# Loading order, transposes and output quotas at the start of a fused convolution and Swish layer

## Chip, cores, metric

One core of a Trainium2 chip; the calls of runs went to several chips. The metric is the device time of one execution in microseconds (us). The timeline is counted from the first instruction.

## Reference

Input x is 8 sequences of 4096 tokens with 192 features. A causal convolution of 7 taps, its weights a softmax per head, mixes tokens; then every token goes through a layer with 2048 hidden units.

```python
w = softmax(weight, axis=-1)                       # [8 heads, 7 taps]
conv[b, s] = sum_k w[head, k] * x_padded[b, s + k] # head = feature // 24
h = conv @ w_in                                    # [32768, 192] @ [192, 2048]
out = (h / (1 + exp(-beta * h))) @ w_out           # [2048, 192]
```

## The kernel before

Work comes in 32 stages. A stage takes one chunk of 512 tokens from each half of the batch. It has 16 units; each computes 128 hidden units for 2 x 512 tokens (6 matmuls into PSUM tile `ph`, then a Silu on ScalarE), and runs output matmuls for hidden units that are already done. Output work is cut into jobs: one job accumulates 256 tokens over all 16 units (32 pairs of matmuls) in a PSUM tile, `pa` or `pb`, and VectorE then reduces that tile to `osb` for the store. Two jobs at most are open, one per tile.

```python
def jobs_of(s):            # four jobs a stage: two batch halves x two token ranges
    ...
def output(s, u, pairs, free):
    for _ in range(pairs):
        for name in free:                       # "a" and "b": the two PSUM tiles
            if slots[name] is None and waiting:
                slots[name] = waiting.popleft()
        ...                                     # the oldest job that has something ready
        if job.pair():                          # two matmuls; true after the 32nd pair
            job.leave()                         # reduction on VectorE, store
            slots[name] = None
```

The convolution of chunk s+2 runs on VectorE during stage s, as 21 operations (taps) that are popped one or two at a time from a queue, between the reductions. It needs the chunk transposed, so a cast load on GpSimd writes the chunk as bf16 to DRAM (`cast`), and a DMA transpose brings it back as features x tokens (`xpose`).

```python
for s in range(N_ST):
    if s == 0:
        queue.extend(conv_ops(1, 1))
    jobs_of(s)
    for u in range(NF):                         # 16 units
        ...                                     # hidden(s, u)
        output(s, u, 8, "a" if s == 0 and u <= CONV1[-1] else "ab")   # CONV1 ends at 10
        ...                                     # pops_u taps from the queue
        if u == 0 and s + 4 < N_CH:
            cast(s + 4)
        if u == 1 and s + 2 < N_CH:
            xpose(s + 2)
            queue.extend(conv_ops(s + 2, 0))
```

The first two chunks are special. Chunk 0 is transposed on TensorE and convolved there. Chunk 1 is loaded, cast on VectorE and sent through four DMA transposes; one of its three column groups is then convolved on TensorE, tap by tap, in units 4 to 10 of stage 0. The casts of later chunks are let go by a small GpSimd copy that waits for the first convolved column of chunk 0:

```python
for b in range(NB):
    nc.sync.dma_start_transpose(
        xt[:, :, HALO + b * BLK : HALO + (b + 1) * BLK],
        x1b[:, b].rearrange("q c h d -> q (c h d)"),
    )
...
        if c == 0:
            nc.gpsimd.tensor_copy(hold, cts[0][0:1, 0, 0:1])
scale_w_out(0)
cast(2)
cast(3)
```

## Time and profile before

| | before |
|---|---|
| median of 3 runs (range) | 716.6 us (716.33 to 718.79) |
| span of the profiled execution | 717.9 us |
| TensorE busy | 695.2 us, 97% |
| stage 0 starts, stage 1 starts | 15.05, 42.29 us |
| last unit ends | 707.0 us |

Part 1 of the page of the kernel before, busy us by engine:

```profile
PE 695.2 (97%) x11320; PEld 521.0 (73%) x11320; DVE 522.5 (73%) x810; ACT 578.7 (81%) x532; POOL 59.6 (8%) x74
```

TensorE bounds it. In the timeline its pattern of 6 hidden and 16 output matmuls repeats every 1.307 us, with no gap, in all undisturbed units; 16 units make 20.92 us and 32 stages 669 us. So the question is where the remaining 49 us go. The two largest entries of what TensorE waited for, in all of the kernel before (us in total, times, longest):

```profile
PE pa L410 <- DVE osb L429: 9.8, 14, 1.1
PE pb L257 <- DVE xt L342: 4.9, 1, 4.9
```

And the two largest of VectorE:

```profile
DVE ct L362 <- DMA xt<-xd: 122.6, 26, 6.1
DVE osb L429 <- PE pa L410: 41.9, 19, 9.2
```

**The single wait of 4.9 us** is in stage 0. TensorE in the timeline of before (start, duration, engine, line, operation, then in brackets the idle time ahead of it and what ended it):

```profile
19.77 0.82 PE L380 MATMUL ph<-ct,w_in_s 64*128 64x512 bf16 x6
25.54 0.79 PE L257 MATMUL pb<-xt,diag 128*128 128x512 f32 x1 [4.94 <-DVE xt L342]
```

The tap needs chunk 1, whose DMA transposes were issued from 14.1 us; VectorE had the last of it at 24.8. The windows view of before for the same stretch (busy us of TensorE, weight loads, VectorE, ScalarE, GpSimd; then granted clock, DMA share, GB/s; the DMA share is the time of all packets over that of the 16 engines, and as packets overlap it can pass 1):

```profile
21.00:22.00 1.00, 0.00 (x0) 0.00 (x0) 0.00 (x0) 0.75 (x1) 1.00 (x2) 1.00 2.44 157
22.00:23.00 1.00, 0.00 (x0) 0.00 (x0) 0.00 (x0) 0.00 (x0) 1.00 (x2) 0.75 2.11 168
23.00:24.00 1.00, 0.00 (x0) 0.00 (x0) 0.00 (x0) 0.00 (x0) 1.00 (x2) 0.50 2.26 148
27.00:28.00 1.00, 1.00 (x7) 0.16 (x3) 1.00 (x3) 0.00 (x0) 0.17 (x1) 0.50 1.40 242
```

TensorE is idle, the DMA share is above 2, and the granted clock falls to 0.50 and stays there after work has resumed. The Trainium skill, "TensorE: Matmul & The Clock Gate", Part 1 ("The HAM clock gate"), says that an idle window of about 3.4 us puts the array at half clock. The trace agrees in part. The idle time here, 4.94 us, is longer than that and the clock did fall; but the windows view in steps of 0.25 us has it fall at 22.5 us, only 1.9 us after TensorE's last matmul (20.6).

**The 14 short waits** are at stage boundaries. VectorE, then TensorE, in the timeline of before, near the start of a later stage:

```profile
228.18 8.03 DVE L364 SCALAR_TENSOR_TENSOR ct<-xt,cw,ct 128x512 bf16<-128x512 bf16 x12
236.13 0.95 DVE L429 TENSOR_REDUCE osb<-pa 128x384 f32<-128x768 f32 x1
237.00 0.95 DVE L429 TENSOR_REDUCE osb<-pb 128x384 f32<-128x768 f32 x1
242.79 0.88 DVE L362 TENSOR_SCALAR ct<-xt,cw 128x512 bf16<-128x512 bf16 x3 [4.85 <-DMA xt<-xd]
```

```profile
235.18 0.83 PE L380 MATMUL ph<-ct,w_in_s 64*128 64x512 bf16 x6
237.14 0.84 PE L410 MATMUL pa<-w_out_s,g 64*128 64x192 bf16 x16 [1.12 <-DVE osb L429]
```

Two things meet. The jobs in `pa` and `pb` finish in the same unit, so both tiles wait for a reduction and the next job has none. And VectorE works in order (the same page, in the paragraph "Engine queue depths", calls it a strict FIFO; this trace agrees: the reductions start at 236.13 us, when the 12 taps of 8.03 us ahead of them are out): it had stood idle for a transpose at the start of the stage, was behind with its taps, and the reductions came late. Even a stage that shows no such wait takes 21.17 us, not 20.92. The DMA transposes of before, issued once a stage at the same place:

```profile
67.04 3.81 SPq L113 DMA_TRANSPOSE xt<-xd  x1
88.21 4.15 SPq L113 DMA_TRANSPOSE xt<-xd  x1
```

### The profile page before, as it was taken

The page shows a single profiled execution, that of the slowest core. Times are in us where ns is not written, and L with a number is a line of the kernel's source. Part 1 is how long each engine was busy: PE and PEld are TensorE (multiplying, and loading weights), DVE is VectorE, ACT ScalarE, POOL GpSimd, SP SyncE. Part 2 cuts the span into 40 slices and gives each one's busy share as a digit, 9 for nine tenths or more (in the row PEclk, how much of TensorE's full clock was granted, in tenths as well). Part 3 has the DMA queues.
Part 4 walks back from the last instruction along what each step waited for, and adds up shares of the span by engine and source line. Part 5 has one row for each costly group of instructions (what it writes and reads, how often), then busy time and mean ns, then how long its engine had stood idle before and what let it go on. Part 6 is the DMA issues. An engine that isn't in the chain of part 4 may idle for free.

```text
span 717.9 us, 24618 instructions
## 1 busy us (share of the span) xinstructions
PE 695.2 (97%) x11320; PEld 521.0 (73%) x11320; DVE 522.5 (73%) x810; ACT 578.7 (81%) x532; POOL 59.6 (8%) x74
## 2 busy tenths in 40 slices
PE   8799999999999999999999999999999999999997
PEld 5377777777777777777777777777777777777776
DVE  5588888987886777887766887667887677797321
ACT  5588888888888788887888888887888878888884
POOL 4555442000000000000000000000000000000000
PEclk9899999999999999999999999999999999999999
DMA  8999999522113222312223112332212322213111
GB/s 189 170 164 172 163 175 173 82 57 59 51 42 70 68 57 57 54 40 68 69 57 58 56 38 69 68 58 57 53 40 69 68 57 59 59 39 63 46 35 57
DMA packets 185784, 55.35 MB, mean 77 GB/s; under 512 B 148032, under 2 KB 185680, under 8 KB 185680
## 3 DMA queue, kind: packets, MB, share of 16 engines
q0 software_dynamic: 96544, 12.92, 27.5%
q1 hardware_dynamic: 89088, 40.85, 24.9%
q8 instruction: 88, 1.44, 0.9%
q14 instruction: 16, 0.13, 0.1%
q10 hardware_dynamic: 48, 0.01, 0.0%
HBM read 28.98 MB, written 37.29 MB: 92 GB/s over the span
## 4 chain that ended last, share of the span: by engine, by line
PE 37%; DVE 31%; DMA 24%; issue 4%; POOL 1%; SPq 1%; ACT 0%
DVE ct L364 22%; PE ph L380 17%; DMA xd<-in_x_dram 12%; DMA xt<-xd 11%; PE pa L410 10%; PE pb L410 9%; DVE osb L429 8%; DMA x<-in_x_dram 1%; DVE ct L362 1%; POOL xd L104 1%; SPq L437 1%; SPq L140 0%; ACT g L388 0%; DVE ct L318 0%; DVE x1b L299 0%
## 5 line engine op out<-in xcount | busy, mean ns | idle before, releaser
L388 ACT ACTIVATE g<-ph,beta 128x1024 bf16<-128x1024 f32 x512 | 570.2, 1114 | 121.5 <-PE ph L380 117.5
L410 PEld LDWEIGHTS <-g 64*128 64x128 bf16 x8192 | 368.0, 94 | 123.4 <-issue 22.7
L380 PE MATMUL ph<-ct,w_in_s 64*128 64x512 bf16 x3072 | 424.2, 377 | 0.3 <-ACT g L388 0.2
L364 DVE SCALAR_TENSOR_TENSOR ct<-xt,cw,ct 128x512 bf16<-128x512 bf16 x552 | 371.7, 745 | 0.0
L410 PE MATMUL pa<-w_out_s,g 64*128 64x192 bf16 x4128 | 240.6, 243 | 11.5 <-DVE osb L429 9.8
L410 PE MATMUL pb<-w_out_s,g 64*128 64x192 bf16 x4064 | 224.5, 243 | 0.0
L380 PEld LDWEIGHTS <-w_in_s 64*128 64x128 bf16 x3072 | 158.5, 94 | 54.3 <-issue 1.6
L362 DVE TENSOR_SCALAR ct<-xt,cw 128x512 bf16<-128x512 bf16 x92 | 27.8, 354 | 122.7 <-DMA xt<-xd 122.6
L429 DVE TENSOR_REDUCE osb<-pa 128x384 f32<-128x768 f32 x64 | 61.0, 954 | 41.9 <-PE pa L410 41.9
L429 DVE TENSOR_REDUCE osb<-pb 128x384 f32<-128x768 f32 x63 | 59.9, 950 | 10.2 <-PE pb L410 10.2
L104 POOL DMA_DIRECT2D xd<-in_x_dram x60 | 54.6, 912 | 45.0 <-DMA xd<-in_x_dram 43.3
L257 PE MATMUL pb<-xt,diag 128*128 128x512 f32 x7 | 4.1, 584 | 4.9 <-DVE xt L342 4.9
L257 PEld LDWEIGHTS pb<-xt,diag 128*128 128x128 f32 x7 | 1.5, 215 | 8.4 <-DVE xt L342 5.4
L257 PE MATMUL ph<-xt,diag 128*128 128x512 f32 x14 | 5.4, 562 | 0.1
L257 PEld LDWEIGHTS ph<-xt,diag 128*128 128x128 f32 x14 | 4.0, 294 | 1.5 <-ACT xt L271 0.5
L320 ACT ACTIVATE ct<-pa,rn 128x512 bf16<-128x512 f32 x1 | 0.7, 688 | 5.3 <-PE pa L257 5.3
L426 ACT COPY osb<-pb 128x192 f32<-128x192 f32 x1 | 0.3, 320 | 5.6 <-PE pb L410 5.6
L288 DVE TENSOR_TENSOR w_out_s<-w_out_raw,beta_r 128x768 bf16<-128x768 f32 x4 | 3.8, 954 | 0.9 <-DMA w_out_raw<-in_moe_w_out_dram 0.9
L342 DVE CAST xt<-xt 128x518 fp32r<-128x518 bf16 x1 | 0.7, 699 | 5.1 <-DMA xt<-x1b 5.1
L210 PE MATMUL ph<-zeros 128*128 128x512 bf16 x6 | 2.9, 623 | 1.3 <-DVE warm L154 1.3
L188 DVE COPY w_in_s<-w_in_s 64x1536 bf16<-64x1536 bf16 x4 | 2.7, 686 | 0.9 <-DMA w_in_s<-in_moe_w_in_dram 0.8
L350 DVE TENSOR_SCALAR ct<-pb,rn 128x512 bf16<-128x512 f32 x1 | 0.8, 751 | 2.9 <-PE pb L257 2.9
(54 smaller groups left out, 33.3 us busy)
## 6 DMA issues: line engine op xcount, KB each, us to landing
out_dram<-osb SPq DMA_DIRECT2D x127, 192.0 KB, 2.1
xd<-in_x_dram POOLq DMA_DIRECT2D x54, 198.0 KB, 14.7
w_out_raw<-in_moe_w_out_dram SPq DMA_DIRECT2D x4, 384.0 KB, 9.6
xd<-in_x_dram POOLq DMA_DIRECT2D x6, 192.0 KB, 11.1
x<-in_x_dram SPq DMA_DIRECT2D x4, 192.0 KB, 3.3
x<-in_x_dram SPq DMA_DIRECT2D x2, 384.0 KB, 9.1
w_in_s<-in_moe_w_in_dram POOLq DMA_DIRECT2D x4, 192.0 KB, 9.4
xt<-xd SPq DMA_TRANSPOSE x30, 4.7
```

The source lines that it names most:

```text
L104: nc.gpsimd.dma_start(out=xd[r0:, :, h, :], in_=x_v[p, t0:t1, h, :].rearrange("t (c d) -> t c d", c=NG),)
L188: nc.vector.tensor_copy(w_in_s[DG : 2 * DG, :, cols], w_in_s[0:DG, :, cols])
L210: nc.tensor.matmul(pf[:, 0, 0:cols], zeros[:, 0:128], zeros[:, 0:cols], start=True, stop=True)
L257: nc.tensor.matmul(pv, diag[:, c, k, :], xt[:, o : o + TOK], start=(k == 0), stop=(k == K - 1))
L288: nc.vector.tensor_tensor(w_out_s[:, fcs, :], w_out_raw[:, fcs, :], beta_r[:, fcs].unsqueeze(2).to_broadcast((128, NQ, D)), ALU.mult,)
L362: nc.vector.tensor_scalar_mul(dst, src, scalar)
L364: nc.vector.scalar_tensor_tensor(out=dst, in0=src, scalar=scalar, in1=dst, op0=ALU.mult, op1=ALU.add)
L380: nc.tensor.matmul(ph[:, h, :], w_in_s[rows, j, fc * 128 : (fc + 1) * 128], cts[s][rows, j, :], start=(j == 0), stop=(j == NG - 1),)
L388: nc.scalar.activation(gs[s][:, fc], ph, AF.Silu, scale=beta[:, fc : fc + 1])
L410: nc.tensor.matmul(self.po[:, r, b * D : (b + 1) * D], g[rows, fc, self.h, q * BLK : (q + 1) * BLK], w_out_s[rows, fc, :], start=(self.don ...
L429: nc.vector.tensor_reduce(dst, self.po[:, :, 0 : nb * D].rearrange("p r n -> p n r"), axis=mybir.AxisListType.X, op=ALU.add,)
L437: nc.sync.dma_start(out=out_v[self.h, p, t : t + nb * BLK, :].rearrange("(b q) d -> q b d", q=BLK), in_=osb[:, 0:nb, :],)
```

## The change

Its intent: get chunk 1 to TensorE sooner (transpose it there, not by DMA), load the first rows in longer pieces, keep other loads out of the way, and have later transposes done before VectorE asks for them. It also lowers the output quotas of stage 0. The core of the diff (cuts marked):

```diff
-    for b in range(NB):                                   # x0: four loads, 768-byte rows
-        nc.sync.dma_start(...)
+    def load_x(dst, t0):                                  # x0, x1: two loads each, 1536-byte rows
+        for i in range(2):
+            ...  "(q b) h d -> q h (b d)", b=2
...
-    for i in range(NW):
-        load_w_in(i)
+    load_w_in(0)
...                                                        # after the conv weights are spread:
+    nc.gpsimd.tensor_copy(hold[:, 0:1], eu[0:1, 0, 0:1])
+    for i in range(1, NW):
+        load_w_in(i)
...
-        nc.sync.dma_start_transpose(...)                  # chunk 1, four times
+    def second():                                         # chunk 1, in units 1 and 2; casts in unit 3
+        ...
+            for b in range(2):
+                transposes(halves[i][:, :, b], x1b, 2 * i + b)     # TensorE
+            nc.vector.tensor_copy(...)                             # PSUM to xt
+            ...
+        nc.gpsimd.tensor_copy(hold[:, 1:2], xt[0:1, 0, HALO + TOK - 1 :])
+        cast(2)
+        cast(3)
...
-            output(s, u, 8, "a" if s == 0 and u <= CONV1[-1] else "ab")
+            if s > 0:
+                output(s, u, 8, "ab")
+            elif u > CONV1[-1]:
+                output(s, u, 5, "ab")
+            elif u > 2:
+                output(s, u, 3, "a")
...
-            if u == 1 and s + 2 < N_CH:
-                xpose(s + 2)
+            if u == 1 and s > 0 and s + 3 < N_CH:
+                xpose(s + 3)
+            ...                                           # stage 0: xpose(2) in unit 4, xpose(3) in unit 12
+            if u == 4 and s + 2 < N_CH:
                 queue.extend(conv_ops(s + 2, 0))
```

Not shown: two of the four `w_out` loads move forward, short `fill` matmuls are added at the start, and some weight copies change place.

More of the change, by code (lines that the diff above doesn't have):

```diff
@@ L120 @@
     NQ = NF // NW
-    x0 = setup.tile([128, NB, 2, D], FP32)
-    x1 = setup.tile([128, NB, 2, D], FP32)
+    x0 = setup.tile([128, 2, 2, 2, D], FP32)
+    x1 = setup.tile([128, 2, 2, 2, D], FP32)
     x0b = setup.tile([128, NB, NG, 2, DG], BF16)
@@ L138 @@
     nc.scalar.dma_start(out=cw8, in_=weight)
-    for b in range(NB):
-        nc.sync.dma_start(
-            out=x0[:, b, :, :], in_=x_v[0, b * BLK : (b + 1) * BLK, :, :]
-        )
-    for h in range(2):
-        nc.sync.dma_start(
-            out=x1[:, :, h, :],
-            in_=x_v[0, TOK : 2 * TOK, h, :].rearrange("(b q) d -> q b d", q=BLK),
-        )
-    load_w_out(0)
-    load_w_out(1)
+    def load_x(dst, t0):
+        for i in range(2):
+            t = t0 + i * 2 * BLK
+            nc.sync.dma_start(
+                out=dst[:, i].rearrange("q h b d -> q h (b d)"),
+                in_=x_v[0, t : t + 2 * BLK, :, :].rearrange(
+                    "(q b) h d -> q h (b d)", b=2
+                ),
+            )
+    load_x(x0, 0)
+    load_x(x1, TOK)
+    for i in range(NW):
+        load_w_out(i)
     zeros = setup.tile([128, TOK], BF16)
@@ L214, with spread, cast_rows, transposes @@
     NK = NG * (K + 1)
-    def spread(dst, sel, e8):
-        for c in range(NG):
-            nc.tensor.matmul(
-                dst[:, c * (K + 1) : (c + 1) * (K + 1)],
-                sel[:, c, :, :].rearrange("i h d -> i (h d)"),
-                e8,
-                start=True,
-                stop=True,
-            )
+    def spread(dst, sel, e8, c):
+        nc.tensor.matmul(
+            dst[:, c * (K + 1) : (c + 1) * (K + 1)],
+            sel[:, c, :, :].rearrange("i h d -> i (h d)"),
+            e8,
+            start=True,
+            stop=True,
+        )
+    def cast_rows(xb, x, b):
+        nc.vector.tensor_copy(
+            xb[:, b].rearrange("q c h d -> q h c d"),
+            x[:, b // 2, :, b % 2].rearrange("q h (c d) -> q h c d", c=NG),
+        )
+    def transposes(pt, xb, b):
+        for c in range(NG):
+            nc.tensor.transpose(
+                pt[:, c, :], xb[:, b, c].rearrange("q h d -> q (h d)"), ident_b
+            )
+    def tokens(xt, b):
+        t = HALO + (b // 2) * 2 * BLK
+        return xt[:, :, t : t + 2 * BLK].rearrange("p c (q b) -> p c b q", b=2)[:, :, b % 2]
     fill(5)
     pc = in_a()
-    spread(pc[:, 0, :], sel_r, e8r)
+    for c in range(NG):
+        spread(pc[:, 0, :], sel_r, e8r, c)
+        fill(1, 256)
     for b in range(NB):
-        nc.vector.tensor_copy(
-            x0b[:, b].rearrange("q c h d -> q h c d"),
-            x0[:, b].rearrange("q h (c d) -> q h c d", c=NG),
-        )
+        cast_rows(x0b, x0, b)
     eu = setup.tile([128, NG, K + 1], FP32)
     nc.vector.tensor_copy(eu.rearrange("p c k -> p (c k)"), pc[:, 0, 0:NK])
+    hold = setup.tile([1, 2], FP32)
+    nc.gpsimd.tensor_copy(hold[:, 0:1], eu[0:1, 0, 0:1])
+    for i in range(1, NW):
+        load_w_in(i)
     diag = setup.tile([128, NG, K, 128], FP32R)
@@ L266 @@
         pt = pts[b % 2][:, b // 2, 0 : NG * BLK].rearrange("p (c q) -> p c q", c=NG)
-        for c in range(NG):
-            nc.tensor.transpose(
-                pt[:, c, :], x0b[:, b, c].rearrange("q h d -> q (h d)"), ident_b
-            )
-        nc.scalar.copy(xt0[:, :, HALO + b * BLK : HALO + (b + 1) * BLK], pt)
+        transposes(pt, x0b, b)
+        nc.scalar.copy(tokens(xt0, b), pt)
+        fill(1, 128)
     pb = pc[:, 1, 0:NF]
@@ L295 @@
     copy_w_in(0)
-    xt = new_xt(1)
-    for h in range(2):
-        nc.vector.tensor_copy(
-            x1b[:, :, :, h, :], x1[:, :, h, :].rearrange("q b (c d) -> q b c d", c=NG)
-        )
-    nc.vector.tensor_copy(xt[:, :, HALO - PAD : HALO], xt0[:, :, HALO + TOK - PAD :])
-    for b in range(NB):
-        nc.sync.dma_start_transpose(
-            xt[:, :, HALO + b * BLK : HALO + (b + 1) * BLK],
-            x1b[:, b].rearrange("q c h d -> q (c h d)"),
-        )
-    load_w_out(2)
-    load_w_out(3)
-    hold = setup.tile([1, 1], BF16)
     new_ct(0)
@@ L321 @@
         if c == 0:
-            nc.gpsimd.tensor_copy(hold, cts[0][0:1, 0, 0:1])
-    scale_w_out(0)
-    cast(2)
-    cast(3)
+            for b in range(NB):
+                cast_rows(x1b, x1, b)
     cw = consts.tile([128, NG, K], FP32)
-    def taps():
+    def second():
+        xt = new_xt(1)
+        pt = in_b()
+        halves = [
+            pt[:, i, 0 : NG * BLK].bitcast(BF16).rearrange(
+                "p (c b q) -> p c b q", c=NG, b=2
+            )
+            for i in range(2)
+        ]
+        for i in range(2):
+            for b in range(2):
+                transposes(halves[i][:, :, b], x1b, 2 * i + b)
+            t = HALO + i * 2 * BLK
+            nc.vector.tensor_copy(
+                xt[:, :, t : t + 2 * BLK].rearrange("p c (q b) -> p c q b", b=2),
+                halves[i].rearrange("p c b q -> p c q b"),
+            )
+            if i == 0:
+                nc.vector.tensor_copy(
+                    xt[:, :, HALO - PAD : HALO], xt0[:, :, HALO + TOK - PAD :]
+                )
+                scale_w_out(0)
+            yield
+        nc.gpsimd.tensor_copy(hold[:, 1:2], xt[0:1, 0, HALO + TOK - 1 :])
+        cast(2)
+        cast(3)
         pq = in_b()[:, 0, 0:NK]
-        spread(pq, sel, e8)
+        for c in range(NG):
+            spread(pq, sel, e8, c)
         pq = pq.rearrange("p (c k) -> p c k", c=NG)
+        copy_w_in(1)
         rq = setup.tile([128, NG], FP32)
@@ L338, in taps @@
         )
+        yield
     def conv1():
@@ L474, in output @@
                 slots[name] = None
+    second_work = second()
     conv1_work = conv1()
     first_work = {
-        1: lambda: (copy_w_in(1), scale_w_out(1)),
+        4: lambda: scale_w_out(1),
         5: lambda: copy_w_in(2),
@@ L499 @@
                     hidden(0, fc, range(NG - 1, NG), phs[fc])
-            else:
-                taps()
+            if s == 0 and 0 < u < 4:
+                next(second_work)
             if s == 0 and u in CONV1:
                 next(conv1_work)
-            output(s, u, 8, "a" if s == 0 and u <= CONV1[-1] else "ab")
+            if s > 0:
[4 more added lines that the diff above has]
+                output(s, u, 3, "a")
             if s == 0 and u in first_work:
@@ L514 @@
                     queue.popleft()()
-            if u == 0 and s + 4 < N_CH:
+            if u == 0 and s > 0 and s + 4 < N_CH:
                 cast(s + 4)
-            if u == 1 and s + 2 < N_CH:
-                xpose(s + 2)
+            if u == 1 and s > 0 and s + 3 < N_CH:
+                xpose(s + 3)
+            if s == 0 and u == 4:
+                xpose(2)
+                cast(4)
+            if s == 0 and u == 12:
+                xpose(3)
+            if u == 4 and s + 2 < N_CH:
                 queue.extend(conv_ops(s + 2, 0))
```

## The prediction

> **What bounds it now.** TensorE: the page gives it 695.2 of 717.9 us busy (97%). In an undisturbed stage the timeline shows one unit (6 hidden, 16 output matmuls) every 1.307 us; the Silu needs 1.11 us (groups). 16 units are 20.92 us, so 32 stages have a floor of 669 us; the rest is start, tail and waits.
>
> **Where time is lost.**
> 1. Start. The timeline has TensorE idle from 20.6 to 25.5 us (waits: "DVE xt" 4.9 us): the second chunk goes through four DMA transposes (issued 14.1, landed 24.8) while loads hold the DMA share above 1.4 (windows). The granted clock is then 0.50 for some 6.8 us. The Trainium skill, "TensorE: Matmul & The Clock Gate", Part 1, says an idle window of about 3.4 us halves the clock; this trace agrees. Stage 0 starts at 15.05, stage 1 at 42.3.
> 2. Stage boundaries. Vector idles 122.6 us in 26 waits for xt<-xd, because the transpose is issued just before its taps enter Vector's in-order queue; it then runs 12 taps without a break (8.0 us), and the PSUM reductions come late. Two output jobs also finish in the same unit of every stage, so the next must wait for a reduction. Waits list 9.8 us in 14 for "PE pa <- DVE osb", up to 1.1 us. The good stages too take 21.17 us, not 20.92 (transpose issues), 0.25 us lost at this place. From stage 1 to the end of the last unit (707.0) it takes 664.7 us for 31 stages, 16.2 us over 31 x 20.92.
>
> **What changes.**
> - x0/x1: larger rows, fewer issues, three w_in loads held back: stage 0 starts near 14.3.
> - Second chunk: 12 TensorE transposes (about 0.17 us each, partly in Silu-bound units, nearly free), two Vector copies of about 0.9 us. Vector should have xt1 near 21.3, so a stall of about 1.5 us stays, likely too short to lose the clock. Units 5 to 10 stay at 1.35 us; units 11 to 15 carry 5 output pairs, not 8, so near 1.1 us. Stage 1 starts near 36.0: gain 6.3 us.
> - The 15 output pairs not done in stage 0 move to the tail: +1.3 us at 0.088 us each, partly returned by a lost 0.7 us reduction wait there: +0.4 net.
> - Transposes a stage sooner, taps entering at unit 4, and, through the changed backlog, reductions at units 0, 2, 6, 10 (instruction order): no two adjacent, each over two units before its bank is wanted. I expect 15.7 of the 16.2 us back.
> Vector is not the limit (16.5 of 21 us a stage).
>
> **Sum.** Span 717.9 - 6.3 - 15.7 + 0.4 = 696.3; the unprofiled median lies 1.3 below: 695 us. Range 690.5 to 701. Chances: faster by over 2% 0.90, within 2% 0.09, slower 0.01.
>
> **What would show it.** Waits: "PE pa <- DVE osb" below 1.5 us; "DVE ct <- DMA xt<-xd" below 8 us, all near the start; transposes issued every 20.9 us; stage 1 near 36; clock at 1.00 from 22 to 29 us; tail about 11.4 us.
>
> **What would make it wrong.** Held-back w_in or the later casts (issued near 20, not 15 us) arrive late, and Vector, in order, blocks in stage 0 or on chunk 2: 2 to 4 us lost. The stall near 20 us stays long enough to halve the clock. Or the stage boundary has another limit than reductions: then a stage stays at 21.17 and the time is near 702.

## The result

697.66 us, median of 4 runs (696.41 to 698.47), against 717.69 (716.33 to 720.02) in 4 runs of before. The ratio is 0.9716, 95% interval 0.9683 to 0.9749. Ratios are computed as the mean time of one kernel's fast runs over that of the other's of the same rounds, so not quite the ratio of the medians. Later line numbers shift: L441, L411, L460, L393 after are L410, L380, L429, L362 before.

Part 1 of the page, after:

```profile
PE 688.6 (99%) x11339; PEld 497.9 (71%) x11339; DVE 528.2 (76%) x814; ACT 578.5 (83%) x532; POOL 60.6 (9%) x75
```

What TensorE waited for, after. The reductions are gone from the list, the wait for chunk 1 is down to 0.3 us (the last line), and a wait for beta is new:

```profile
PE pa L293 <- DMA beta_q<-in_moe_beta_dram: 1.4, 1, 1.4
PE ph L213 <- DVE warm L158: 1.3, 1, 1.3
PE ph L411 <- ACT g L419: 0.6, 1, 0.6
PE pa L441 <- ACT g L419: 0.4, 1, 0.4
PE pb L220 <- DVE xt L346: 0.3, 1, 0.3
```

What VectorE waited for, after. It now idles for its reductions' inputs, which costs nothing:

```profile
DVE osb L460 <- PE pa L441: 121.5, 61, 6.8
DVE ct L393 <- DMA xt<-xd: 0.2, 1, 0.2
```

TensorE around the first tap of chunk 1, after, and two of the same windows:

```profile
21.38 0.81 PE L411 MATMUL ph<-ct,w_in_s 64*128 64x512 bf16 x6
22.12 0.50 PE L279 MATMUL pb<-xt,diag 128*128 128x512 f32 x1
```

```profile
22.00:23.00 1.00, 1.00 (x11) 0.55 (x11) 1.00 (x2) 0.77 (x1) 1.00 (x2) 1.00 1.02 66
23.00:24.00 1.00, 1.00 (x9) 0.31 (x7) 0.97 (x2) 0.68 (x2) 1.00 (x2) 1.00 2.27 145
```

No wait there, and the clock stays at 1.00. The reductions in a later stage, after, are no longer neighbours of each other:

```profile
225.81 0.96 DVE L460 TENSOR_REDUCE osb<-pa 128x384 f32<-128x768 f32 x1 [0.85 <-PE pa L441]
226.68 2.07 DVE L395 SCALAR_TENSOR_TENSOR ct<-xt,cw,ct 128x512 bf16<-128x512 bf16 x3
228.67 0.95 DVE L460 TENSOR_REDUCE osb<-pb 128x384 f32<-128x768 f32 x1
```

And the transposes of after are issued every 20.92 us:

```profile
227.27 1.45 SPq L113 DMA_TRANSPOSE xt<-xd  x1
248.19 1.44 SPq L113 DMA_TRANSPOSE xt<-xd  x1
```

In sections, from the timelines of the two profiled executions:

| section | before | predicted | after |
|---|---|---|---|
| to the start of stage 0 | 15.05 | 14.3 | 15.58 |
| stage 0 | 27.24 | 21.7 | 20.60 |
| stages 1 to 31 | 664.7 | 649.0 | 648.7 |
| tail | 10.9 | 11.4 | 11.8 |
| span | 717.9 | 696.3 | 696.7 |

The span came out as predicted, in part because two errors cancel (see below). And the change bundles six edits, and two theories that share a total can differ on which edits earn it. The prediction itself credited the middle row to "transposes a stage sooner" and the backlog together, and the stage-0 row to the TensorE transposes. The experiments separate these.

### The profile page after: what moved, and what is told of

Read it like the earlier page. It is cut to its first block, busy times and chain, and to the rows that moved or that the text cites. A ratio compares the mean times of both kernels' runs of the same rounds, so it can differ in the third digit from the quotient of the medians.

```text
span 696.7 us, 24650 instructions
## 1 busy us (share of the span) xinstructions
PE 688.6 (99%) x11339; PEld 497.9 (71%) x11339; DVE 528.2 (76%) x814; ACT 578.5 (83%) x532; POOL 60.6 (9%) x75
## 4 chain that ended last, share of the span: by engine, by line
PE 98%; DMA 1%; ACT 0%; DVE 0%; issue 0%; ACTq 0%
PE ph L411 47%; PE pa L441 25%; PE pb L441 24%; DMA beta_q<-in_moe_beta_dram 1%; PE ph L279 1%; PE pb L279 0%; PE pa L279 0%; ACT g L419 0%; ACT L159 0%; DVE xt L346 0%; DVE w_out_s L308 0%; PE pb L220 0%; ACTq L138 0%; PE ph L213 0%; PE pb L237 0%
## 5 line engine op out<-in xcount | busy, mean ns | idle before, releaser
L441 PEld LDWEIGHTS <-g 64*128 64x128 bf16 x8192 | 352.3, 94 | 121.2 <-issue 1.7
L411 PE MATMUL ph<-ct,w_in_s 64*128 64x512 bf16 x3072 | 415.1, 376 | 0.6 <-ACT g L419 0.6
L395 DVE SCALAR_TENSOR_TENSOR ct<-xt,cw,ct 128x512 bf16<-128x512 bf16 x552 | 375.9, 745 | 0.0
L441 PE MATMUL pa<-w_out_s,g 64*128 64x192 bf16 x4128 | 234.1, 243 | 0.4 <-ACT g L419 0.4
L441 PE MATMUL pb<-w_out_s,g 64*128 64x192 bf16 x4064 | 224.5, 243 | 0.0
L411 PEld LDWEIGHTS <-w_in_s 64*128 64x128 bf16 x3072 | 141.9, 94 | 62.0 <-issue 0.9
L460 DVE TENSOR_REDUCE osb<-pa 128x384 f32<-128x768 f32 x64 | 61.3, 958 | 121.9 <-PE pa L441 121.5
L460 DVE TENSOR_REDUCE osb<-pb 128x384 f32<-128x768 f32 x63 | 60.0, 953 | 31.2 <-PE pb L441 31.1
L393 DVE TENSOR_SCALAR ct<-xt,cw 128x512 bf16<-128x512 bf16 x92 | 30.3, 359 | 0.2 <-DMA xt<-xd 0.2
L213 PE MATMUL ph<-zeros 128*128 128x512 bf16 (+2 forms) x13 | 5.3, 475 | 1.3 <-DVE warm L158 1.3
L346 DVE COPY xt<-pb 128x768 bf16<-128x768 bf16 x2 | 1.9, 958 | 2.6 <-PE pb L237 2.6
L213 PEld LDWEIGHTS <-zeros 128*128 128x128 bf16 x13 | 1.6, 129 | 2.2 <-DVE warm L158 1.3
```

The source lines that it names most:

```text
L213: nc.tensor.matmul(pf[:, 0, 0:cols], zeros[:, 0:128], zeros[:, 0:cols], start=True, stop=True)
L346: nc.vector.tensor_copy(xt[:, :, t : t + 2 * BLK].rearrange("p c (q b) -> p c q b", b=2), halves[i].rearrange("p c b q -> p c q b"),)
L393: nc.vector.tensor_scalar_mul(dst, src, scalar)
L395: nc.vector.scalar_tensor_tensor(out=dst, in0=src, scalar=scalar, in1=dst, op0=ALU.mult, op1=ALU.add)
L411: nc.tensor.matmul(ph[:, h, :], w_in_s[rows, j, fc * 128 : (fc + 1) * 128], cts[s][rows, j, :], start=(j == 0), stop=(j == NG - 1),)
L441: nc.tensor.matmul(self.po[:, r, b * D : (b + 1) * D], g[rows, fc, self.h, q * BLK : (q + 1) * BLK], w_out_s[rows, fc, :], start=(self.don ...
```

## Experiments

Kernels named `a_` are edits of the changed kernel, `b_` of the kernel before; `after_again` is the changed kernel itself. All twelve runs gave correct results. Medians are compared within one call (same chip, same rounds) where that is possible. The changed kernel itself ran only in the first and the last call, so its comparison with the other `a_` kernels crosses calls. The kernel before had medians of 717.7 to 720.7 us.

### Stage boundaries: quota or earlier transposes?

**a_quota8**

```diff
-                output(s, u, 5, "ab")
+                output(s, u, 8, "ab")
```

> The changed kernel, with 8 output pairs instead of 5 in units 11 to 15 of stage 0, everything else kept (early transposes, TensorE transposes, held loads). Theory BACKLOG (the backlog that the smaller quota leaves staggers the PSUM reductions, and that stagger is what removes the wait at stage boundaries): two reductions are adjacent again in every stage, each of 31 stages loses 0.25 us again (period 21.17, not 20.92), stage 0 is about 1.2 us longer and the tail about 0.6 us shorter: 704 to 706 us, about 7.5 over the changed kernel's 697.7; no stage loses over 0.4 us, because Vector isn't blocked by a transpose. Rival SOONER (only the earlier transposes matter): 697 to 699 us, period 20.92.

Measured: 705.14 us (704.77 to 705.47), ratio to before 0.9803. The transposes, still early, are issued every 21.17 us. VectorE and TensorE at a stage boundary of a_quota8:

```profile
206.42 0.96 DVE L460 TENSOR_REDUCE osb<-pa 128x384 f32<-128x768 f32 x1 [1.22 <-PE pa L441]
207.30 0.95 DVE L460 TENSOR_REDUCE osb<-pb 128x384 f32<-128x768 f32 x1
208.16 2.07 DVE L395 SCALAR_TENSOR_TENSOR ct<-xt,cw,ct 128x512 bf16<-128x512 bf16 x3
```

```profile
206.54 0.83 PE L411 MATMUL ph<-ct,w_in_s 64*128 64x512 bf16 x6
207.43 0.84 PE L441 MATMUL pa<-w_out_s,g 64*128 64x192 bf16 x16
208.09 0.83 PE L411 MATMUL ph<-ct,w_in_s 64*128 64x512 bf16 x6
```

The two reductions are neighbours again, though VectorE was idle and took the first at once. The next job starts when that reduction is out (206.42 + 0.96 = 207.38), and the unit takes 1.55 us, not 1.307. The waits view does not list this, because the modelled ends of the pipelined matmuls cover the gap; the start times show it.

**a_late**

```diff
-            if u == 1 and s > 0 and s + 3 < N_CH:
-                xpose(s + 3)
+            if u == 1 and s > 0 and s + 2 < N_CH:
+                xpose(s + 2)
+                queue.extend(conv_ops(s + 2, 0))
...
-            if s == 0 and u == 12:
-                xpose(3)
-            if u == 4 and s + 2 < N_CH:
+            if u == 4 and s == 0:
                 queue.extend(conv_ops(s + 2, 0))
```

> The changed kernel, with the transposes from stage 1 on issued as in the kernel before (chunk s+2 in unit 1 of stage s, its taps entering at the same place), the quota of 5 kept. BACKLOG: Vector idles again about 4 us a stage for the transposed chunk (over 100 us in all), but no TensorE wait comes of it, because each bank is free two units before it is wanted: 697 to 699.5 us, period 20.92. SOONER: the waits come back, 8 to 16 us more, 705 to 714 us.

Measured: 697.93 us (697.83 to 698.88), 0.3 us over the changed kernel's median. VectorE and TensorE waits of a_late:

```profile
DVE ct L393 <- DMA xt<-xd: 65.6, 27, 5.5
```

```profile
PE pa L441 <- DVE osb L460: 0.5, 1, 0.5
PE pb L441 <- DVE osb L460: 0.3, 1, 0.3
```

VectorE waits for transposes again (65.6 us, less than the 100 expected, because part of the time now goes to reductions that come in between: its waits for their inputs are 89.5 us, against 52.1 before). In this view TensorE loses 0.8 us by it. The start times show somewhat more: stages 5 and 6 take 22.09 and 21.21 us, together 1.5 us over twice 20.92, and no later stage loses anything. TensorE in stage 5 of a_late, behind the longest of VectorE's waits above (5.5 us, to 131.4):

```profile
132.94 0.42 PE L441 MATMUL pa<-w_out_s,g 64*128 64x192 bf16 x6 [0.49 <-DVE osb L460]
```

The transpose that VectorE waited for there was issued at 120.9 us, so it took 10.5 us, while casts were still running (the last landed at 133.5 us). The next four, with no casts left, took 3.9 to 5.1 us. The time of this execution (698.03 us, against 698.47 of the changed kernel's) does not show the 1.5 us, because its stage 0 started at 13.71 us and not at 15.58.

**b_quota5**: in the kernel before, only the output line is replaced by the six lines of the diff above.

> The kernel before, with only the output quotas of stage 0 changed (3 pairs up to unit 10, 5 pairs in units 11 to 15). BACKLOG: the whole loss at stage boundaries goes (16 us), stage 0 about 1.2 us shorter, tail 0.6 us longer: 700 to 703 us, against 717.7; the stall of 4.9 us near 21 us and the half clock stay; Vector still idles about 120 us for transposes. SOONER: 715 to 718 us.

Measured: 702.92 us (702.06 to 703.93), against 720.65 for the kernel before: 17.7 us from one changed rule. The stall of stage 0 stays (3.7 us in this profile, clock 0.50 after it), "PE pa <- DVE osb" is gone from the waits, and all stages from stage 2 on take 20.92 us. VectorE still waits 57.1 us for transposes, half of the 120 expected.

```profile
PE pb L257 <- DVE xt L342: 3.7, 1, 3.7
DVE ct L362 <- DMA xt<-xd: 57.1, 26, 3.3
```

**b_early**: in the kernel before, only the transposes from stage 1 on a stage sooner, with the taps entering at unit 4.

> The kernel before, with only the transposes from stage 1 on issued a stage sooner and the taps entering at unit 4; old quota of 8. BACKLOG: the irregular part of the loss goes (8 of 16 us: the waits of up to 1.1 us), the 0.25 us a stage stay: 708 to 711 us, period 21.17 everywhere. SOONER: all 16 us go, 700 to 703 us.

Measured: 710.90 us (709.42 to 713.72), 9.8 us under the kernel before. Transposes are issued every 21.17 us; "PE pa <- DVE osb" is down to one wait of 0.7 us, in the tail. The 0.25 us a stage stay, as in a_quota8.

What follows. The four kernels and the two originals form a square: earlier transposes earn 9.8 us with the old quotas and 0.3 us with the new ones (1.5 us by the stages of the profiles); the new quotas earn 17.7 us alone and 7.5 us on top of early transposes. The two are partly two ways to the same waits, and only the quota removes the 0.25 us that every stage loses. The rival SOONER is refuted by a_late and b_quota5.

Why 5 works where 8 doesn't, from the job arithmetic. A job can have done 28 of its 32 pairs by the end of its stage, because two units are not yet ready. With 8 pairs a unit in units 11 to 15, both open jobs get to 28 (56 pairs in stage 0). Each lacks 4, and both finish in the first unit of the next stage, leaving no tile for the next job. With 5 (43 pairs in stage 0), the younger job stands at 15 and lacks 17, two units of work, and a reduction of 0.96 us fits in. The backlog is set once, in stage 0; every later stage adds and removes 128 pairs, so the stagger persists. (The count is read from the scheduler and agrees with the order of reductions in the traces; no run varied the quota to values other than 5 and 8.)

### The stall of stage 0: which path, or which neighbours?

**a_dma_held**: the changed kernel with chunk 1 through DMA transposes. x1 takes back its row layout and its two loads.

```diff
+            for b in range(NB):
+                nc.sync.dma_start_transpose(
+                    xt_1[:, :, HALO + b * BLK : HALO + (b + 1) * BLK],
+                    x1b[:, b].rearrange("q c h d -> q (c h d)"),
+                )
...                                   # in second():
-                transposes(halves[i][:, :, b], x1b, 2 * i + b)
-            nc.vector.tensor_copy(...)
```

> The changed kernel, with the second chunk transposed by four DMA transposes as in the kernel before (row layout of x1 as before for that), but the later casts still held until that chunk has landed. Theory CONTENTION (the DMA transposes were late before because casts and weight loads filled the DMA engines): with the casts held they land near 21 us, TensorE waits 1 to 2 us there, no half clock: 698 to 700.5 us. Rival PATH (the DMA path is too slow by itself, four serial issues of 1.3 us and a landing of about 5 us, whatever else runs): they land after 23 us, a wait of 3 us or more, the clock falls: 701 to 705 us.

Measured: 695.64 us (695.52 to 696.02). This is better than either theory expected. The TensorE wait and two windows of a_dma_held:

```profile
PE pb L283 <- DVE xt L371: 0.4, 1, 0.4
```

```profile
18.00:20.00 2.00, 1.56 (x17) 0.92 (x16) 1.14 (x4) 1.35 (x2) 0.84 (x2) 1.00 0.26 48
22.00:24.00 2.00, 2.00 (x18) 0.77 (x14) 2.00 (x4) 1.54 (x2) 2.00 (x4) 1.00 2.15 135
```

**a_dma_nohold**: as a_dma_held, but `hold` waits for the first convolved column, and the casts follow at once, as before.

> As a_dma_held, with the casts let go as early as in the kernel before (when the first conv column is out, near 12 us). CONTENTION: landing at 23 to 25 us, TensorE wait of 3.5 to 5 us, clock at 0.50 after it: 701 to 705 us, so 3 us or more over a_dma_held. PATH: equal to a_dma_held within 1 us.

Measured: 703.05 us (702.84 to 703.27), 7.4 over a_dma_held. The same two views of a_dma_nohold:

```profile
PE pb L283 <- DVE xt L371: 5.5, 1, 5.5
```

```profile
18.00:20.00 2.00, 2.00 (x22) 1.20 (x18) 0.36 (x2) 1.53 (x2) 2.00 (x3) 1.00 2.19 156
22.00:24.00 2.00, 0.00 (x0) 0.00 (x0) 0.00 (x0) 0.00 (x0) 0.90 (x1) 0.65 1.83 154
```

With the casts held, the DMA engines are at a share of 0.26 at 18 to 20 us, the four transposes take a median of 3.9 us to land, and chunk 1 is there at 19.2 us. With the casts running, the share is 2.19, landing takes 7.2 us, chunk 1 comes at 24.6 us, TensorE waits 5.5 us and loses its clock. CONTENTION holds and PATH is refuted. The edit moves one wait, so the casts are the cause. (The transposes are also issued 0.9 us later in a_dma_nohold, at 13.6 us, which is little of the 5.4 us by which they land later.)

**a_pe_nohold**: the changed kernel (TensorE transposes) with only the casts let go early.

> The changed kernel (TensorE transposes), with only the casts let go early, near 12 us. If holding them matters only for a chunk that goes through DMA transposes: 696 to 699 us, no wait of TensorE beyond 1 us near 21 us, as in the changed kernel. If the early casts delay w_in or w_out so that Vector blocks in stage 0: 699 to 702 us.

Measured: 697.33 us (697.01 to 699.20); the only wait near 21 us is of 0.3 us, clock 1.00. So with TensorE transposes it does not matter when the casts start.

The second square: TensorE path, casts held 697.66 and early 697.33; DMA path, held 695.64 and early 703.05. Either the held casts or the TensorE transposes remove the stall. The change has both and needs one. That a_dma_held beats the changed kernel by 2.0 us at the median (its ranges do not touch those of a_pe_nohold and a_beta_first) is not explained: in the profile its stage 0 starts at 13.31 us and stage 1 at 33.84, the same as in the control run of the changed kernel below (13.25 and 33.85), and only the tail is 0.6 us shorter.

One thing narrows this. Taken from the start of stage 0 to the end, three profiled executions of TensorE-transposing kernels agree to 0.1 us: 698.47 - 15.58 (the changed kernel), 696.13 - 13.25 (after_again) and 699.20 - 16.35 (a_pe_nohold) are all 682.9 us. So the 3.1 us between these executions arose before stage 0. The same difference for a_dma_held is 682.2 us. The rest of its 2.0 us would have to be a start that is early in most executions, which one profile can't show.

### The start: rows, held weights, beta

The step "stage 0 starts near 14.3" did not come true in the profile after, where TensorE, in order, waited for beta (landing 6.1 us after issue, before 2.8 us).

**a_beta_first**: the load of beta moved right behind that of the conv weights.

```diff
     nc.scalar.dma_start(out=cw8, in_=weight)
+    nc.scalar.dma_start(out=beta_q, in_=moe_beta.rearrange("(c p) -> c p", p=128))
```

> The changed kernel, with the load of beta issued right behind that of the conv weights (near 1.4 us) and not behind the exponential (2.6 us). In the profile after, beta landed 6.1 us after its issue and TensorE, in order, waited 1.4 us for it ahead of the first taps, so that stage 0 started at 15.6 us and not at the 14.3 predicted. If that wait is what failed: first taps near 7.9 us, stage 0 at 13.7 to 14.3, no wait for beta in the profile, 694.5 to 697 us unprofiled. If the wait is rare in unprofiled runs: no difference, 697 to 698 us.

Measured: 697.50 us (696.88 to 697.64, 6 runs). In its profile beta lands in 3.0 us, nothing waits for it, and stage 0 starts at 13.90. But the time is the same, so a late beta is not what the median of the changed kernel loses. My guess missed.

**a_w_in_up**: all four w_in loads issued at the start, as before.

> The changed kernel, with all four w_in loads issued at the start as in the kernel before, not held behind the conv weights. Theory: they take DMA time from x0 and x1, so the first taps come 0.5 to 1 us later: stage 0 at 14.5 to 15.5 us, 698 to 699 us. Rival: the DMA engines serve x0 first anyway, no difference: 697 to 698 us.

Measured: 696.55 us (696.41 to 696.87), stage 0 at 13.56 us. **a_rows**: x0 and x1 loaded one token per row, eight loads.

> The changed kernel, with x0 and x1 loaded one token in a row per partition (eight loads of 768-byte rows, not four of 1536). Theory: more issues and smaller rows let x0 land about 0.5 us later: stage 0 at 14.2 to 15 us, 697.5 to 699 us. Rival: x0 lands as soon, and beta, behind smaller packets, lands sooner: 696 to 697.5 us.

Measured: 696.37 us (696.13 to 697.07); stage 0 at 15.20 us in the profile. Both rivals fit better: neither the held w_in nor the longer rows earns anything that can be seen. Undoing them is, if anything, about 1 us faster, but a profile's start of stage 0 (13.25 to 15.58 us for one and the same kernel) is too loose to settle 1 us. What holds up the start in most executions stays open.

### Two edits alone

**b_quota5_held**: the kernel before, with the output quotas, and with the casts held until chunk 1 is transposed.

```diff
-        if c == 0:
-            nc.gpsimd.tensor_copy(hold, cts[0][0:1, 0, 0:1])
+    nc.gpsimd.tensor_copy(hold, xt[0:1, 0, HALO + TOK - 1 :])
...                                   # and the output lines as in b_quota5
```

> The kernel before with two edits alone: the output quotas of stage 0 (3 and 5 pairs), and the casts of chunks 2 and later held until the second chunk has come through its DMA transposes. Row layout, w_in loads, DMA transposes of the second chunk and the place of all later transposes as before. Theory TWO PARTS (the staggered reductions and the quiet DMA engines around the second chunk are all that the change earns): the wait for xt1 falls from about 4 us to under 1.5 us, the clock stays at 1.00, period 20.92: 696.5 to 699 us, equal to the changed kernel within 1.5 us. If rows, held w_in, TensorE transposes or earlier transposes earn something of their own: 700 us or more.

**after_again**: the changed kernel, unedited, in the same rounds.

> Control: the changed kernel itself, unedited, on the chip of b_quota5_held and in its rounds. 696 to 698.5 us, as on the first chip. Its profile also shows whether the wait of 1.4 us for beta is of every execution: a landing of beta under 5 us and no wait would make it chance.

Measured: b_quota5_held 699.24 us (697.00 to 701.15, 6 runs), after_again 697.20 us (696.13 to 697.56, 4 runs), the kernel before 720.42. So the two edits earn 21.2 of the 23.2 us. The other four share 2.0 us, a little over the 1.5 us expected and 0.2 over the top of the range. The waits of b_quota5_held that matter here:

```profile
PE ph L379 <- DVE ct L318: 1.7, 2, 1.5
PE pa L409 <- DVE osb L428: 1.2, 1, 1.2
PE pb L257 <- DVE xt L341: 0.4, 1, 0.4
```

The stall for xt is down to 0.4 us. The 1.5 us are a late x1 (in this kernel the casts of x1 stand ahead of the first convolved column in VectorE's queue, and x1 was there at 14.96 us); the 1.2 us are one late reduction. The first is of this one profile. The second is what a_late showed, in the same place, in stage 5 (TensorE waits at 135.9 us), behind the longest wait of VectorE in this view:

```profile
DVE ct L361 <- DMA xt<-xd: 72.4, 28, 5.9
```

Stages 5 and 6 take 22.82 and 21.21 us, 2.2 us over twice 20.92. Both kernels combine late transposes with held casts. b_quota5, with late transposes and early casts (the last landed at 128.3 us), takes 20.92 us in both stages, and so does the changed kernel, with early transposes and held casts. So, beside held casts, the earlier transposes earn part of the 2.0 us; how much of it in most executions, these single profiles don't tell. In the profile of after_again beta landed in 4.4 us with no wait, and stage 0 started at 13.25 us: the wait of 1.4 us in the first profile was chance.

| kernel | median us | lowest to highest | ratio to before |
|---|---|---|---|
| changed kernel, first | 697.66 | 696.41 to 698.47 | 0.9716 |
| after_again | 697.20 | 696.13 to 697.56 | 0.9674 |
| a_quota8 | 705.14 | 704.77 to 705.47 | 0.9803 |
| a_late | 697.93 | 697.83 to 698.88 | 0.9706 |
| b_quota5 | 702.92 | 702.06 to 703.93 | 0.9773 |
| b_early | 710.90 | 709.42 to 713.72 | 0.9888 |
| a_dma_held | 695.64 | 695.52 to 696.02 | 0.9670 |
| a_dma_nohold | 703.05 | 702.84 to 703.27 | 0.9772 |
| a_pe_nohold | 697.33 | 697.01 to 699.20 | 0.9698 |
| a_beta_first | 697.50 | 696.88 to 697.64 | 0.9693 |
| a_w_in_up | 696.55 | 696.41 to 696.87 | 0.9690 |
| a_rows | 696.37 | 696.13 to 697.07 | 0.9690 |
| b_quota5_held | 699.24 | 697.00 to 701.15 | 0.9700 |

The fastest is a_dma_held: the changed kernel without its TensorE transposes. It beats both originals at the median, by 0.3% over the changed kernel.

## Why the prediction was right, and where it was not

- **Stage boundaries: right in size and in mechanism.** 15.7 of 16.2 us predicted back, and 664.7 - 648.7 = 16.0 measured. The named mechanism (reductions at units 0, 2, 6, 10 through the changed backlog) is the one that a_quota8, a_late and b_quota5 confirm. But the step listed "transposes a stage sooner" first, as a partner. With the new quotas they earn 0.3 us of the time, and 1.5 us by the stages of a_late's profile.
- **Stage 0: right in outcome, on a cause that is enough but not the only one.** "A stall of about 1.5 us stays" was mis-sized: 0.3 us, so stage 0 took 20.6 us and not 21.7. The prediction credited the TensorE transposes, and a_pe_nohold shows that they are enough with the casts early. What it did not see is that the casts were what made the DMA path late: a_dma_held shows that holding them does it as well, without TensorE transposes.
- **"x0/x1: larger rows, fewer issues, three w_in loads held back: stage 0 starts near 14.3": not shown.** 15.58 and 13.25 us in two profiles of the same kernel, against 15.05 before; undoing either edit costs nothing.
- **Tail: 11.4 predicted, 11.8 measured**, so 0.9 us longer than before and not 0.4 to 0.5. The moved output pairs are 13, by the count above, not the 15 that I had taken.
- **The span: right, in part by luck.** It was predicted as 696.3 and came out as 696.7, but stage 0 started 1.3 us later than predicted and took 1.1 us less, and these two errors cancel. The start is also a matter of the execution: with stage 0 at 13.25 us, after_again has a span of 694.4.
- **"The unprofiled median lies 1.3 below": the worst term of the sum.** A time is 1.7 to 1.8 us above its span. The profile of before was of an execution of 719.69 us, the slowest then, and I took the difference of its span to the median for a constant. Median minus span should have been near +1, not -1.3; that is most of the 2.7 us between 695 and 697.66.
- Of the feared failures (late w_in or casts blocking VectorE, the clock, another limit at the boundary) none appeared in the changed kernel. a_dma_nohold shows what a long stall and the clock cost together: 7.4 us, with a wait of 5.5.

## What to carry to other kernels

When two accumulators share one in-order engine for their drain, look at whether they finish together; moving one of them by a unit of work, once, at the start, can remove a wait from every later stage. A late producer may cost little if the consumer behind it has slack, so test it by making it late again before spending work on it. And before giving a slow transfer a new path, look at what else is in the DMA engines at that time: here a wait on the neighbours' issue did as much as the new path. Last, compare sections of profiles before explaining differences of 1 or 2 us: here the start alone moved by 3 us.

## What the Trainium skill lacked or had wrong

- "TensorE: Matmul & The Clock Gate", Part 4 (PE-mode transpose), gives about 390 ns for a 128x128 bf16 transpose on TensorE in isolation and about 275 ns in a kernel. In the profile after, each of the 12 transposes of chunk 1 takes 219 to 230 ns by the trace's modelled ends, at a granted clock of 1.00. What this passage doesn't give is how they overlap: they start about 56 ns apart, so that six in a row take 0.51 us.
- "VectorE: DVE Perf Modes", "The three transpose paths", puts the DMA path at 1309 ns for a 128x128 block and says nothing of load. Here four DMA transposes of 128x384 each landed 3.9 us after issue at the median with the casts held and 7.2 us with casts running, and which of the two decided 7.4 us of the kernel's time.
- "DMA: Bandwidth & Descriptors" says under "Rules for kernel authors" that a transpose next to ordinary DMAs needs nothing. That is about correctness; no page has what it costs in time, which the same 3.9 and 7.2 us show. So do the later transposes of a_late: 10.0 to 11.1 us from issue to landing in stages 1 to 4, beside casts, and 3.9 to 5.1 us in stages 6 to 9, after them.
- No page has it that an execution takes 1.7 to 1.8 us more than the span of its profile, as every profiled run here shows.
